# First product of the state tokens in three rounded products for chunks 1 to 3, with the batch sums moved to the front of a batch's last step

## The chip, the cores and the metric

One core of a Trainium2 chip runs the whole program. The metric is the device time of one execution in microseconds (us); the number that stands for a kernel is the median of several executions. One more execution was recorded by the hardware profiler, and all rows below come from it.

## The reference

Three layers follow each other. All inputs and outputs are fp32, and the kernel keeps fp32 accuracy.

```python
xread = softmax(scale * x @ state.T) @ state          # 4 batches, 8 heads, 512 tokens, D = 64
sread = softmax(scale * state @ x.T) @ x              # 32 state tokens per batch
x = concat([xread, sread])                            # 2304 tokens x 512
h = x @ w_in; g = softplus(h); x = g @ w_out          # first layer, d_ff = 2048
g = x @ w_gate; x = (silu(g) * (x @ w_val)) @ w_out2  # second layer, d_ff = 1536
```

Of the 2304 tokens 2048 come from `x` and 128 rows (4 batches x 32) come from `state`. Only these 128 state rows are touched by the first part of the change, and only in the product `x @ w_in`.

## The kernel before, in words

**Numbers in two parts.** A matrix is split into a high part (a float32r copy, made by ACT) and a low part (the rest, a subtraction on POOL or DVE, `low`, line 92). `mm3` (line 86) multiplies two split matrices with three float32r matmuls: high by high, low by high, high by low. A matmul on plain fp32 operands needs no split, and is recorded as two rows on PE.

**Weights** come as 64-bit words. A `Piece` of 128 x 512 goes through steps: a load (SP), `size` (ACT, line 132), `head` (DVE, line 136), `tail` (two integer passes on DVE, lines 143 and 146); these leave the fp32 tile `t_...`. Then come `high` (ACT, line 152) and `low` (POOL, line 92). Pieces of `w_in` end at `tail`; pieces of `w_out` go to the end. In between, pieces of the second layer (`gv`, `w`) are converted early and stored to memory; a `gv` piece is followed by four `sums` on POOL (line 193), a high part of them (`split_gv`, ACT, line 197) and a low part (POOL).

**The first layer** runs over four chunks c = 0 to 3 of 512 columns of d_ff, and in each over four batches b and four slices ft of 128: 64 units, 16 to a chunk and 4 to a batch. A unit has a first product `p1` (`ph`, six matmuls), the softplus twice (ACT `h` and `C`), their difference `l` (POOL, `g_low`), and a second product `p2` (`py`, twelve matmuls: four quarters dt of the output, three each). `p2` adds over the four slices of a batch in four PSUM banks; after a batch's last slice `y_add` (line 444) adds each quarter to `yacc` on DVE (line 453), which frees the bank.

**The order** is written by hand. The main loop goes over units n; at each step PE has `p2(n)`, the hooks called "pe", `p1(n + 4)`. Then ACT has `h` and `C` of the unit n + 3, and the other engines have their hooks: "dve0", "act", then `l`, "pool", "dve1", "act1". A table of hooks says at which step of a chunk something comes; each engine works through its own list in this order. SBUF slots and PSUM banks are given out by a planner, so more tiles of a kind can be alive than `bufs` says.

`p1` does not read the tokens' rows of w_in directly but a product `m` of state and w_in: `pm` (16 small matmuls, line 374) for the next chunk comes at steps 10, 12, 15 and 19 of a chunk (`M_STEPS`), with its high part on ACT and its low part on DVE one step later.

**The state tokens** go beside this, once per chunk: `s1` (line 502) multiplies `sw`, the 128 state rows, with the chunk's `w_in` in four plain fp32 matmuls (line 505) into `ps`; `s1_first` (line 508) takes the softplus, `sps`; `s2` turns it (`ptgs`), `s2_high` and `s2_low` split it into `gs`; `s3` (line 524) multiplies by `w_out` in twelve float32r matmuls, `ps<-wo,gs`; `s4` adds to `ys`. `s1` of chunk c + 1 stands at step 10 of chunk c, right behind `pm`; `s3` at step 20.

The lines of the main loop that the change moves:

```python
run(n, "dve0")
for dt in range(2) if last else ():
    y_add(u[0], u[1], dt)
run(n, "act")
if nx:
    g_low(nx)
run(n, "pool")
for dt in range(2, KT) if last else ():
    y_add(u[0], u[1], dt)
```

Of the kernel before, what the change touches and what calls it, by code (L numbers as in the profile page):

```python
# [9 lines left out]
F32R = mybir.dt.float32r  # L10
# [6 lines left out]
P = 128  # L17
# [16 lines left out]
FIRST = 9  # L34
# [3 lines left out]
def attention_moe_moe2_kernel(  # L38
# [36 lines left out]

    SLOTS = {"aT": 8, "mt": 8,  "wo": 6, "yacc": 8, "s": 2, "xT": 8, "T": 14, "made": 3, "w2": 4, "gw": 8}

# [162 lines left out]
    aT = {}  # L240
    sw = const.tile([P, KT, P], F32, tag="yo", name="sw")
    sr = {}
    srp = {}
# [118 lines left out]
    def st_out(b):  # L362
        v = srp[b][:, :P].rearrange("p (k s) -> p k s", k=KT)
        nc.scalar.activation(sw[:, :, b * NS:(b + 1) * NS], v, AF.Copy)


# [135 lines left out]
    def s1(c):  # L502
        ps = bank("m", f"ps1{c}")
        for kt in range(KT):
            nc.tensor.matmul(ps, sw[:, kt, :], win[c, kt].t, start=kt == 0, stop=kt == KT - 1)  # L505
        sp["s", c] = Softplus(ps, slot([P, CH], F32, "s", f"sps{c}"), None)
# [144 lines left out]
    with tc.manual_schedule(engines={ENG.PE}):  # L651
# [70 lines left out]
        def at_weights(n, late, store, key, make):  # L722
# [4 lines left out]
            for m, kind, step in (  # L727
                (n - 1, "act1", "size"), (n, "dve0", "head"), (n + late, "dve1", "tail"),
                (n + late + 1, "act", "high"), (n + late + 1, "pool", "low"),
            )[:3 if store is win else 5]:  # L730
                if m == FIRST - 1 and n == FIRST:
# [4 lines left out]
        for c in range(NCK):  # L736
# [15 lines left out]
            if c + 1 < NCK:  # L752
                for i, kind, fn in (
                    (10, "pe", s1), (11, "act", s1_first), (16, "pe", s2), (16, "act", s2_high), (17, "dve0", s2_low),
                    (20, "pe", s3), (21, "dve0", s4),
                ):
                    at(n0 + i, kind, fn, c + 1)
# [17 lines left out]
        for i in range(2):  # L775
# [4 lines left out]
            for k, t in ((0, "B22"), (1, "T1"), (2, "T3"), (3, "T2"), (4, "T4")):  # L780
                at(n0 + 2 * i + k, "act", y_high, 0, i, t)
                if t in ("T1", "T2", "T3"):
                    at(n0 + 2 * i + k + 1, "dve0", y_low, 0, i, t, nc.vector)
                else:
                    at(n0 + 2 * i + k, "pool", y_low, 0, i, t, nc.gpsimd)
        at(NU - 4, "pe", turn_ys)
        for n in range(2):
# [3 lines left out]
        with tc.manual_schedule(engines={ENG.DVE, ENG.SP, ENG.Activation, ENG.Pool}):  # L791
# [5 lines left out]
            for n in range(FIRST, NU):  # L797
# [10 lines left out]
                if nx:  # L808
                    sp[nx].high()
                    sp[nx].whole()  # L810
                last = u[2] == FT - 1
                run(n, "dve0")
                for dt in range(2) if last else ():
                    y_add(u[0], u[1], dt)
                run(n, "act")
                if nx:
                    g_low(nx)
                run(n, "pool")
                for dt in range(2, KT) if last else ():
                    y_add(u[0], u[1], dt)  # L820
                run(n, "dve1")
# [146 lines left out]
```

## Time and profile before

| what | value |
|---|---|
| median of 3 runs | 749.46 us (749.22 to 749.99) |
| the profiled execution | 746.57 us |
| its span | 744.8 us |
| mean granted clock of PE | 0.999 |
| busy: PE, POOL, DVE, ACT | 718.5, 384.4, 427.9, 321.5 us |
| first layer's `p2`, first to last | about 57 to 349 us |

PE is the row to read first: it is busy for 96% of the span. An idle stretch of another engine matters only if PE, or a chain that PE waits for, runs through it. Times such as 164.73 are microseconds from the start of the span.

### The profile page before, as it was taken

The page shows a single profiled execution, that of the slowest core. Times are in us where ns is not written, and L with a number is a line of the kernel's source. Part 1 is how long each engine was busy: PE and PEld are TensorE (multiplying, and loading weights), DVE is VectorE, ACT ScalarE, POOL GpSimd, SP SyncE. Part 2 cuts the span into 40 slices and gives each one's busy share as a digit, 9 for nine tenths or more (in the row PEclk, how much of TensorE's full clock was granted, in tenths as well). Part 3 has the DMA queues.
Part 4 walks back from the last instruction along what each step waited for, and adds up shares of the span by engine and source line. Part 5 has one row for each costly group of instructions (what it writes and reads, how often), then busy time and mean ns, then how long its engine had stood idle before and what let it go on. Part 6 is the DMA issues. An engine that isn't in the chain of part 4 may idle for free.

```text
span 744.8 us, 9985 instructions
## 1 busy us (share of the span) xinstructions
PE 718.5 (96%) x3640; PEld 566.9 (76%) x3640; DVE 427.9 (57%) x605; ACT 321.5 (43%) x586; POOL 384.4 (52%) x352
## 2 busy tenths in 40 slices
PE   5699999999999999999999999999999999999997
PEld 1367767776778777788788877888888888888885
DVE  5984558878666866467665555554644333333334
ACT  3766455543555454544543453442442232223221
POOL 2467637786648755744875566574442232223222
PEclk9999999999999999999999999999999999999999
DMA  9930224654545544460498988787455846255402
GB/s 337 408 118 5 80 86 141 199 198 169 168 143 177 191 127 157 164 260 1 165 378 295 333 326 310 255 320 244 142 198 184 274 174 226 88 200 205 161 1 113
DMA packets 51072, 143.78 MB, mean 193 GB/s; under 512 B 5712, under 2 KB 18000, under 8 KB 51024
## 3 DMA queue, kind: packets, MB, share of 16 engines
q1 hardware_dynamic: 51024, 143.15, 54.7%
q8 instruction: 28, 0.46, 0.2%
q14 instruction: 20, 0.16, 0.1%
HBM read 107.22 MB, written 35.91 MB: 192 GB/s over the span
## 4 chain that ended last, share of the span: by engine, by line
PE 82%; DVE 6%; DMA 4%; ACT 3%; POOL 3%; issue 2%; SPq 0%; ACTq 0%; DVEq 0%; POOLq 0%
PE py L89 24%; PE px L89 16%; PE po L89 16%; PE ph L89 10%; PE pz L89 7%; PE pt L89 3%; DMA gw<-gv_d 2%; PE ps L505 2%; PE pm L374 2%; DMA raw_gv<-in_moe_w_val_dram 2%; PE ps L89 1%; DMA st<-in_st_dram 1%; POOL sums_gv L193 1%; POOL gv L92 1%; DVE mx L273 1%
## 5 line engine op out<-in xcount | busy, mean ns | idle before, releaser
L89 PE MATMUL py<-h,wo 128*128 128x512 f32 x512 | 158.7, 390 | 2.3 <-DVE yacc L453 1.2
L92 POOL TENSOR_TENSOR l<-C,h 128x512 fp32r<-128x512 f32 x64 | 90.6, 1421 | 88.4 <-ACT C L407 71.7
L89 PE MATMUL po<-w,h 128*128 128x512 f32 x384 | 126.2, 391 | 0.0
L89 PEld LDWEIGHTS py<-h,wo 128*128 128x128 f32 x512 | 95.9, 188 | 23.6 <-POOL wo L92 1.9
L92 POOL TENSOR_TENSOR l<-cA,h 128x512 fp32r<-128x512 f32 x24 | 34.1, 1419 | 147.9 <-ACT h L574 147.9
L89 PE MATMUL ph<-aT,m 128*128 128x512 f32 x384 | 101.2, 399 | 1.5 <-ACT C L407 0.7
L89 PE MATMUL py<-l,wo 128*128 128x512 f32 x256 | 99.9, 390 | 0.1
L89 PEld LDWEIGHTS ph<-aT,m 128*128 128x128 f32 x384 | 70.7, 188 | 25.4 <-issue 6.9
L595 DVE TENSOR_TENSOR oacc<-po,oacc 128x512 f32<-128x512 f32 x80 | 55.1, 690 | 60.2 <-PE po L89 60.0
L404 ACT ACTIVATE h<-ph 128x512 fp32r<-128x512 f32 x64 | 38.2, 596 | 119.5 <-PE py L89 111.7
L89 PEld LDWEIGHTS po<-w,h 128*128 128x128 f32 x384 | 72.1, 188 | 14.9
L89 PE MATMUL po<-w,l 128*128 128x512 f32 x192 | 74.8, 390 | 0.5 <-POOL l L92 0.5
L89 PE MATMUL px<-T_0s,gw 128*128 128x512 f32 x216 | 61.3, 392 | 2.9 <-ACT cC L905 1.4
L89 PE MATMUL px<-T_1s,gw 128*128 128x512 f32 x216 | 60.7, 389 | 0.0
L89 PEld LDWEIGHTS py<-l,wo 128*128 128x128 f32 x256 | 48.0, 188 | 10.7 <-POOL l L92 0.5
L894 DVE TENSOR_TENSOR cA<-py,cA 128x512 f32<-128x512 f32 x24 | 16.6, 691 | 58.0 <-PE py L89 55.8
L89 PEld LDWEIGHTS px<-T_0s,gw 128*128 128x128 f32 x216 | 40.0, 188 | 12.8 <-ACT cC L905 2.3
L574 ACT ACTIVATE h<-cA 128x512 fp32r<-128x512 f32 x24 | 15.1, 631 | 77.7 <-DVE cA L913 77.7
L89 PEld LDWEIGHTS px<-T_1s,gw 128*128 128x128 f32 x216 | 40.5, 188 | 8.5
L905 ACT ACTIVATE cC<-px 128x512 f32<-128x512 f32 x24 | 14.3, 597 | 65.2 <-PE px L89 61.7
L89 PEld LDWEIGHTS po<-w,l 128*128 128x128 f32 x192 | 36.1, 188 | 8.2 <-POOL l L92 1.0
L92 POOL TENSOR_TENSOR l<-cC,h 128x512 fp32r<-128x512 f32 x24 | 31.9, 1327 | 15.4 <-ACT h L574 15.4
(148 smaller groups left out, 1321.5 us busy)
## 6 DMA issues: line engine op xcount, KB each, us to landing
gw<-gv_d SPq DMA_DIRECT2D x96, 512.0 KB, 6.7
gv_d<-gv SPq DMA_DIRECT2D x24, 512.0 KB, 3.1
gv_d<-split_gv SPq DMA_DIRECT2D x24, 512.0 KB, 3.5
w<-w_d SPq DMA_DIRECT2D x24, 512.0 KB, 9.0
raw_win<-in_moe_w_in_dram SPq DMA_DIRECT2D x16, 512.0 KB, 7.4
raw_wo<-in_moe_w_out_dram SPq DMA_DIRECT2D x16, 512.0 KB, 4.1
raw_gv<-in_moe_w_gate_dram SPq DMA_DIRECT2D x48, 128.0 KB, 4.1
raw_gv<-in_moe_w_val_dram SPq DMA_DIRECT2D x48, 128.0 KB, 3.7
```

The costliest lines, as they stand in the source:

```text
L89: nc.tensor.matmul(o, a[s], b[t], start=first and i == 0, stop=last and i == 2, **k)
L92: eng.tensor_tensor(out=o, in0=whole, in1=high.bitcast(F32), op=ALU.subtract)
L193: nc.gpsimd.tensor_tensor(out=o, in0=x, in1=y, op=op)
L273: nc.vector.tensor_reduce(out=self.mine("mx", 1), in_=self.sc, op=ALU.max, axis=AX.X)
L374: nc.tensor.matmul(ps[k * NS:(k + 1) * NS, :], st[q, k, b, :], win[c, k].t[q, :], start=True, stop=True)
L404: nc.scalar.activation(self.h, self.ps, AF.Softplus)
L505: nc.tensor.matmul(ps, sw[:, kt, :], win[c, kt].t, start=kt == 0, stop=kt == KT - 1)
L574: nc.scalar.activation(h, src, AF.Copy)
L595: nc.vector.tensor_tensor(out=v, in0=ps, in1=v, op=ALU.add)
L894: nc.vector.tensor_tensor(out=c["A"], in0=y, in1=c["A"], op=ALU.add)
L905: nc.scalar.activation(c["C"], x, AF.Copy)
```

## The change

It does four things. (1) For c = 1 to 3, `s1` uses `mm3` with `sws`, the high and low parts of `sw`, and with the high and low parts of the w_in pieces: twelve float32r matmuls in place of four fp32 ones. Chunk 0 stays as it is. (2) So `sw` is split once (ACT and DVE), and the twelve pieces of w_in get their `high` (ACT) and `low` (POOL), in four new SBUF slots; they come one step after a piece's `tail`, not before step 9. (3) `s1` goes from step 10 to 13, with its softplus, and `s2` to `s4` go one step later. (4) At a batch's last step all four `y_add` come ahead of the hooks "dve0".

```diff
--- before.py
+++ after.py
@@ -73,7 +73,7 @@
     psum = ctx.enter_context(tc.tile_pool(name="psum", bufs=1, space=bass.MemoryType.PSUM))
 
 
-    SLOTS = {"aT": 8, "mt": 8,  "wo": 6, "yacc": 8, "s": 2, "xT": 8, "T": 14, "made": 3, "w2": 4, "gw": 8}
+    SLOTS = {"aT": 8, "mt": 8,  "wo": 6, "yacc": 8, "s": 2, "xT": 8, "T": 14, "made": 3, "w2": 4, "gw": 8, "win": 4}
 
     def slot(shape, dt, tag, name):
         return slots.tile(shape, dt, tag=tag, bufs=SLOTS[tag], name=name)
@@ -239,6 +239,7 @@
 
     aT = {}
     sw = const.tile([P, KT, P], F32, tag="yo", name="sw")
+    sws = const.tile([P, 2, KT, P], F32R, name="sws")
     sr = {}
     srp = {}
     small = {}
@@ -362,6 +363,11 @@
     def st_out(b):
         v = srp[b][:, :P].rearrange("p (k s) -> p k s", k=KT)
         nc.scalar.activation(sw[:, :, b * NS:(b + 1) * NS], v, AF.Copy)
+
+    def split_sw():
+        v = sws[:, 0]
+        nc.scalar.activation(v, sw, AF.Copy)
+        low(nc.vector, sws[:, 1], sw, v)
 
 
     mt = {}
@@ -502,7 +508,13 @@
     def s1(c):
         ps = bank("m", f"ps1{c}")
         for kt in range(KT):
-            nc.tensor.matmul(ps, sw[:, kt, :], win[c, kt].t, start=kt == 0, stop=kt == KT - 1)
+            if c == 0:
+                nc.tensor.matmul(ps, sw[:, kt, :], win[c, kt].t, start=kt == 0, stop=kt == KT - 1)
+            else:
+                mm3(
+                    ps, [sws[:, i, kt, :] for i in range(2)], [win[c, kt].out[:, i, :] for i in range(2)],
+                    kt == 0, kt == KT - 1,
+                )
         sp["s", c] = Softplus(ps, slot([P, CH], F32, "s", f"sps{c}"), None)
 
     def s1_first(c):
@@ -727,7 +739,9 @@
             for m, kind, step in (
                 (n - 1, "act1", "size"), (n, "dve0", "head"), (n + late, "dve1", "tail"),
                 (n + late + 1, "act", "high"), (n + late + 1, "pool", "low"),
-            )[:3 if store is win else 5]:
+            ):
+                if store is win and step in ("high", "low"):
+                    m = max(m, FIRST + key[1] // 2)
                 if m == FIRST - 1 and n == FIRST:
                     m, kind = FIRST, "load"
                 if m >= FIRST:
@@ -751,8 +765,8 @@
                     at(n0 + i + 1, "dve0", m_pair_low, c + 1, b)
             if c + 1 < NCK:
                 for i, kind, fn in (
-                    (10, "pe", s1), (11, "act", s1_first), (16, "pe", s2), (16, "act", s2_high), (17, "dve0", s2_low),
-                    (20, "pe", s3), (21, "dve0", s4),
+                    (13, "pe", s1), (13, "act", s1_first), (17, "pe", s2), (17, "act", s2_high), (18, "dve0", s2_low),
+                    (21, "pe", s3), (22, "dve0", s4),
                 ):
                     at(n0 + i, kind, fn, c + 1)
         for i, kind, fn in (
@@ -783,6 +797,7 @@
                     at(n0 + 2 * i + k + 1, "dve0", y_low, 0, i, t, nc.vector)
                 else:
                     at(n0 + 2 * i + k, "pool", y_low, 0, i, t, nc.gpsimd)
+        at(FIRST, "act", split_sw)
         at(NU - 4, "pe", turn_ys)
         for n in range(2):
             at(NU - 5 + n, "load", load_gw, n)
@@ -809,15 +824,13 @@
                     sp[nx].high()
                     sp[nx].whole()
                 last = u[2] == FT - 1
+                for dt in range(KT) if last else ():
+                    y_add(u[0], u[1], dt)
                 run(n, "dve0")
-                for dt in range(2) if last else ():
-                    y_add(u[0], u[1], dt)
                 run(n, "act")
                 if nx:
                     g_low(nx)
                 run(n, "pool")
-                for dt in range(2, KT) if last else ():
-                    y_add(u[0], u[1], dt)
                 run(n, "dve1")
                 run(n, "act1")
                 run(n, "pool1")
```

**PE, chunk 1 of the loop, steps 10 to 13.** Before, `s1` (`ps`) stands between `pm` and the next `p1` (`ph`):

```order
L374 MATMUL pm_0_1_1842<-t_win_2_1567,st 32x512
L374 MATMUL pm_0_1_1842<-t_win_3_1629,st 32x512
L505 MATMUL ps_1847<-t_win_0_1385,sw 128x512
L505 MATMUL ps_1847<-t_win_1_1436,sw 128x512
L505 MATMUL ps_1847<-t_win_2_1567,sw 128x512
L505 MATMUL ps_1847<-t_win_3_1629,sw 128x512
L89 MATMUL ph_3_2_1853<-aT_0_938,m_3_0_1548 128x512 x3
L89 MATMUL ph_3_2_1853<-aT_1_940,m_3_1_1550 128x512 x3
L89 MATMUL py_2_0_1745<-h_2_3_1725,wo_3_1307 128x512 x2
```

And with the change, at the same place, and three steps on:

```order
L380 MATMUL pm_0_1_1877<-t_win_2_1596,st 32x512
L380 MATMUL pm_0_1_1877<-t_win_3_1645,st 32x512
L89 MATMUL ph_3_2_1882<-aT_0_939,m_3_0_1576 128x512 x3
L89 MATMUL ph_3_2_1882<-aT_1_941,m_3_1_1578 128x512 x3
...
L89 MATMUL py_3_3_1957<-l_3_1_1900,wo_1_1155 128x512
L89 MATMUL ps_2018<-win_0_1580,sws 128x512 x3
L89 MATMUL ps_2018<-win_1_1521,sws 128x512 x3
L89 MATMUL ps_2018<-win_2_1765,sws 128x512 x3
L89 MATMUL ps_2018<-win_3_1726,sws 128x512 x3
L89 MATMUL ph_0_1_2032<-aT_0_478,m_0_0_1896 128x512 x3
L89 MATMUL ph_0_1_2032<-aT_1_433,m_0_1_1898 128x512 x3
```

The four fp32 rows are gone from step 10, where `ph` now follows `pm`; four groups of three float32r matmuls stand at step 13, ahead of that step's `ph`.

**DVE and PE, chunk 1, end of the second batch** (`py_1_...` are the sums of that batch, `py_2_...` those of the next; `t_w` and `t_gv` are weights of the second layer). DVE before:

```order
L136 TENSOR_SCALAR t_w_1666<-t_w_1666 128x512
L143 SCALAR_TENSOR_TENSOR t_win_2_1567<-raw_win_2_1387,t_win_2_1567 128x512
L146 SCALAR_TENSOR_TENSOR t_win_2_1567<-raw_win_2_1387,t_win_2_1567 128x512
L143 SCALAR_TENSOR_TENSOR t_w_1666<-raw_w_1471,t_w_1666 128x512
L146 SCALAR_TENSOR_TENSOR t_w_1666<-raw_w_1471,t_w_1666 128x512
L136 TENSOR_SCALAR t_gv_0_1703<-t_gv_0_1703 128x512
L453 TENSOR_TENSOR yacc_0_953<-py_1_0_1571,yacc_0_953 128x512
L453 TENSOR_TENSOR yacc_0_953<-py_1_1_1572,yacc_0_953 128x512
L453 TENSOR_TENSOR yacc_1_955<-py_1_2_1573,yacc_1_955 128x512
L453 TENSOR_TENSOR yacc_1_955<-py_1_3_1574,yacc_1_955 128x512
```

DVE with the change:

```order
L549 TENSOR_TENSOR ys<-ps_1661,ys 128x512
L136 TENSOR_SCALAR t_w_1694<-t_w_1694 128x512
L143 SCALAR_TENSOR_TENSOR t_win_2_1596<-raw_win_2_1410,t_win_2_1596 128x512
L146 SCALAR_TENSOR_TENSOR t_win_2_1596<-raw_win_2_1410,t_win_2_1596 128x512
L143 SCALAR_TENSOR_TENSOR t_w_1694<-raw_w_1493,t_w_1694 128x512
L146 SCALAR_TENSOR_TENSOR t_w_1694<-raw_w_1493,t_w_1694 128x512
L459 TENSOR_TENSOR yacc_0_954<-py_1_0_1600,yacc_0_954 128x512
L459 TENSOR_TENSOR yacc_0_954<-py_1_1_1601,yacc_0_954 128x512
L459 TENSOR_TENSOR yacc_1_956<-py_1_2_1602,yacc_1_956 128x512
L459 TENSOR_TENSOR yacc_1_956<-py_1_3_1603,yacc_1_956 128x512
L136 TENSOR_SCALAR t_gv_0_1735<-t_gv_0_1735 128x512
```

The four `yacc` rows now come ahead of the head of `t_gv`, and `ys` stands here, a step later than it did. On PE the first second product of the next batch, with what it waits for, before:

```order
L89 MATMUL ph_2_3_1717<-aT_1_766,m_2_1_1366 128x512 x3
L89 MATMUL py_2_0_1745<-h_2_0_1608,wo_0_1203 128x512 [waits Activation_49]
L89 MATMUL py_2_0_1745<-h_2_0_1608,wo_0_1203 128x512
L89 MATMUL py_2_0_1745<-l_2_0_1662,wo_0_1203 128x512 [waits Pool_49]
L89 MATMUL py_2_1_1746<-h_2_0_1608,wo_0_1203 128x512 [waits DVE_49]
```

and with the change:

```order
L89 MATMUL ph_2_3_1749<-aT_1_767,m_2_1_1392 128x512 x3
L89 MATMUL py_2_0_1780<-h_2_0_1624,wo_0_1211 128x512 [waits DVE_49]
L89 MATMUL py_2_0_1780<-h_2_0_1624,wo_0_1211 128x512
L89 MATMUL py_2_0_1780<-l_2_0_1690,wo_0_1211 128x512 [waits Pool_49]
L89 MATMUL py_2_1_1781<-h_2_0_1624,wo_0_1211 128x512 [waits DVE_49]
```

The planner has dropped the fifth bank: before, the first quarter `py_2_0` waited for ACT only, and the second quarter for the bank that DVE's first `yacc` frees; now the first quarter itself waits for DVE.

**POOL, the same steps 15 to 23 of chunk 1.** Before:

```order
L92 TENSOR_TENSOR l_1_1_1498<-C_1_1_1459,h_1_1_1460 128x512
L92 TENSOR_TENSOR l_1_2_1554<-C_1_2_1493,h_1_2_1494 128x512
L92 TENSOR_TENSOR gv_0_1552<-t_gv_0_1469,gv_0_1552 128x512
L193 TENSOR_TENSOR sums_gv_0_1558<-t_gv_0_1469 128x128
...
L92 TENSOR_TENSOR split_gv_1_1658<-sums_gv_1_1624,split_gv_1_1658 128x512
L92 TENSOR_TENSOR l_2_0_1662<-C_2_0_1607,h_2_0_1608 128x512
L92 TENSOR_TENSOR l_2_1_1697<-C_2_1_1652,h_2_1_1653 128x512
L92 TENSOR_TENSOR l_2_2_1733<-C_2_2_1692,h_2_2_1693 128x512
L92 TENSOR_TENSOR w_1731<-t_w_1666,w_1731 128x512
```

With the change:

```order
L92 TENSOR_TENSOR win_1_1521<-t_win_1_1452,win_1_1521 128x512
L92 TENSOR_TENSOR l_1_2_1584<-C_1_2_1515,h_1_2_1516 128x512
L92 TENSOR_TENSOR win_0_1580<-t_win_0_1408,win_0_1580 128x512
L92 TENSOR_TENSOR gv_0_1582<-t_gv_0_1491,gv_0_1582 128x512
L193 TENSOR_TENSOR sums_gv_0_1589<-t_gv_0_1491 128x128
...
L92 TENSOR_TENSOR split_gv_1_1686<-sums_gv_1_1640,split_gv_1_1686 128x512
L92 TENSOR_TENSOR l_2_0_1690<-C_2_0_1623,h_2_0_1624 128x512
L92 TENSOR_TENSOR l_2_1_1728<-C_2_1_1681,h_2_1_1682 128x512
L92 TENSOR_TENSOR win_3_1726<-t_win_3_1645,win_3_1726 128x512
L92 TENSOR_TENSOR l_2_2_1769<-C_2_2_1720,h_2_2_1721 128x512
L92 TENSOR_TENSOR win_2_1765<-t_win_2_1596,win_2_1765 128x512
L92 TENSOR_TENSOR w_1767<-t_w_1694,w_1767 128x512
```

The low part of `win_0` stands ahead of the low part of `gv_0`, and that of `win_3` between `l_2_1` and `l_2_2`. Chunk 2 has the same rows; in chunk 0 the four new rows stand behind `l_3_0` and `l_3_1`.

## Rows read from the trace of the kernel before

**Rows 1.** The page: busy time by engine, and the costliest group with its idle time

```profile
PE 718.5 (96%) x3640; PEld 566.9 (76%) x3640; DVE 427.9 (57%) x605; ACT 321.5 (43%) x586; POOL 384.4 (52%) x352
...
L89 PE MATMUL py<-h,wo 128*128 128x512 f32 x512 | 158.7, 390 | 2.3 <-DVE yacc L453 1.2
```

**Rows 2.** The chain of waits, first layer: start us, us, what (chunks 1 and 2)

```profile
179.71 3.63 PE ps L505 x8
183.34 1.38 PE ph L89 x6
...
192.56 1.58 PE ph L89 x6
...
228.45 2.72 PE ps L89 x12
```

**Rows 3.** The same chain at the end of chunk 0

```profile
114.60 0.69 DVE m L92
...
115.34 1.66 PE ph L89 x6
```

**Rows 4.** Timeline of PE, chunk 1: [idle before, and what ended it]

```profile
166.08 0.62 PE L89 MATMUL py<-h,wo 128*128 128x512 f32 x2
...
168.15 0.74 PE L89 MATMUL py<-h,wo 128*128 128x512 f32 x2 [1.23 <-DVE yacc L453]
```

**Rows 5.** The chain of waits that leads to this wait of PE

```profile
147.33 1.84 POOL gv L92
...
155.07 1.70 POOL gv L92
...
160.34 0.99 DVE t_w L136
...
163.07 1.66 DVE t_win L146
164.73 0.61 DVE t_w L143
...
165.97 1.52 DVE t_gv L136
167.50 0.61 DVE yacc L453
```

**Rows 6.** Low and high parts of the w_out pieces: xcount, ns min/median/max

```profile
L92 POOL TENSOR_TENSOR wo<-t_wo,wo x16: 1279/1306/1749, 44.4 to 284.4; 128x512 fp32r<-128x512 f32 x16
...
L152 ACT ACTIVATE wo<-t_wo x16: 632/633/692, 43.5 to 282.9; 128x512 fp32r<-128x512 f32 x16
```

**Rows 7.** Timeline of POOL, chunk 1

```profile
161.00 3.17 POOL L92 TENSOR_TENSOR l<-C,h 128x512 fp32r<-128x512 f32 x2
165.92 1.29 POOL L92 TENSOR_TENSOR l<-C,h 128x512 fp32r<-128x512 f32 x1 [1.75 <-ACT C L407]
```

**Rows 8.** Timelines of DVE, POOL and PE, the same place in chunk 2

```profile
242.58 0.68 DVE L143 SCALAR_TENSOR_TENSOR t_w<-raw_w,t_w 128x512 int32<-128x512 int32 x1
...
243.90 0.42 DVE L136 TENSOR_SCALAR t_gv<-t_gv 128x512 int32<-128x512 int32 x1
244.24 2.48 DVE L453 TENSOR_TENSOR yacc<-py,yacc 128x512 f32<-128x512 f32 x4
...
238.93 3.17 POOL L92 TENSOR_TENSOR l<-C,h 128x512 fp32r<-128x512 f32 x2
244.45 1.31 POOL L92 TENSOR_TENSOR l<-C,h 128x512 fp32r<-128x512 f32 x1 [2.35 <-ACT C L407]
...
244.61 0.62 PE L89 MATMUL py<-h,wo 128*128 128x512 f32 x2
```

**Rows 9.** Timelines of DVE and PE at the first batch's end of chunk 3

```profile
298.08 2.73 DVE L453 TENSOR_TENSOR yacc<-py,yacc 128x512 f32<-128x512 f32 x4 [0.90 <-PE py L89]
302.68 2.74 PE py L89 x12
```

**Rows 10.** The page: issues of loads, KB each, median us from issue to landing

```profile
raw_win<-in_moe_w_in_dram SPq DMA_DIRECT2D x16, 512.0 KB, 7.4
```

## The prediction, made before the changed kernel ran

> **What bounds the kernel now.** I read the page first, for who is busy, then the chain of waits, for what the end hangs on, and then the timelines around the one wait that touches this change. PE is busy for 96% of the span, so time is won by taking work from PE or lost by making PE wait [rows 1]. The costliest group of the first layer shows the wait to look at: `py` stood 1.2 us for DVE's `yacc` [rows 1]. The chain of waits then runs along PE through nearly the whole first layer: the fp32 `s1` is in it for 3.63 us per chunk [rows 2]. It leaves PE for long only in chunk 1, at the end of the second batch: `gv` on POOL, its sums, the second `gv`, `t_w` on DVE, its passes, the head of `t_gv`, `yacc`, and then PE [rows 4, 5]. That is where the change puts new work.
>
> **The sum's base.** The profiled execution took 746.57 us; the median of the runs is 749.46 us, 2.89 us more. The terms below are differences, so I add them to the median. Times such as 165.97 are those of the rows; what PE itself gains is counted once, in the first term.
>
> **First product.** Taken out: 3.63 us of `s1` per chunk; the `ph` behind it took 1.38 us, where a `ph` right behind `pm` took 1.58 us, so 0.20 us come back [rows 2]. Put in: twelve float32r matmuls, the same count and width as `ps<-wo,gs`, which took 2.72 us [rows 2]. That makes -3.63 + 0.20 + 2.72 = -0.71 us per chunk, and three chunks **-2.13 us**. All of it lies on PE's path. If `ph` pays nothing extra, it is -2.73; if the new group pays 0.20 us as well, -1.53.
>
> **Step 13 of chunk 0.** `s1` of chunk 1 now comes where `ph` at 115.34 already stood for DVE's low part of `m`, which began at 114.60 [rows 3]. The bank that this low part frees now goes to `s1`, and `ph` follows it: the same wait with another waiter, **0**. The four low parts on POOL that `s1` needs cost at most 4 x 1.75 = 7 us [rows 6] and stand behind `l_3_0` and `l_3_1`, three steps ahead. Were that cover gone, PE would wait for one of them, 1.3 to 1.75 us.
>
> **New work beside PE.** POOL gets twelve low parts; the nearest row, the same subtraction for w_out, has 1.28 to 1.75 us, median 1.31 [rows 6]: 16 to 21 us in all. ACT gets thirteen copies of about 0.63 us [rows 6], DVE one subtraction of 0.69 us as in [rows 3]. Most lie in idle time of engines that are half empty [rows 1] and cost 0. Two of them per chunk, in chunks 1 and 2, don't.
>
> **The chain in chunk 1.** The low part of `win_0` stands on POOL ahead of that of `gv_0`, the start of the chain at 147.33 [rows 5]. So the chain begins 1.31 us late (1.28 to 1.75, [rows 6]). Some may come back: the two `gv` took 1.84 and 1.70 us [rows 5] where such a subtraction can take 1.28 [rows 6], 0.98 us in all, if they now miss the DVE passes beside them. Bounds 1.28 - 0.98 = 0.30 and 1.75; I take 0.9, with a little under half of it coming back.
>
> Next, `win_3`. DVE's passes on the weights slow down beside POOL: the `t_win` pass at 163.07 took 1.66 us while POOL worked through two `l` from 161.00 to 164.17 [rows 5, 7]; the `t_w` pass at 164.73 took 0.61 us with POOL idle until 165.92 [rows 5, 7]. Now `win_3` and then `l_2_2`, whose input is there at 165.92 [rows 7], fill that idle time. Both `t_w` passes may pay 1.66 - 0.62 = 1.04 us more, the 0.62 being half of 164.73 to 165.97 [rows 5]: 0 to 2.08; here I take 2.08, as both POOL instructions are ready.
>
> Against this, `yacc` no longer waits for the head of `t_gv` (1.52 us, [rows 5]), so it starts at 165.97 + 0.9 + 2.08 = 168.95 in place of 167.50. But the first quarter of `py`, which ran at 166.08 in a fifth bank [rows 4], must now wait too. From the start of `yacc` to PE it was 168.15 - 167.50 = 0.65 us [rows 4, 5]; a quarter of twelve matmuls takes 2.72 / 4 = 0.68. So the second quarter comes at 168.95 + 0.65 + 0.68 = 170.28, where it came at 168.15: **+2.13 us** (from 165.97 + 0.30 + 1.33 = 167.60, -0.55, to 165.97 + 1.75 + 2.08 + 1.33 = 171.13, +2.98).
>
> **The same place in chunk 2.** PE did not wait here: the first quarter ran at 244.61, and the first `yacc` at 244.24 freed the next bank just in time [rows 8]. Now the first quarter needs `yacc`, which follows the `t_w` passes that ended at 243.90 [rows 8]. Late by 0.9 from `win_0`; the first pass pays 1.04 beside `win_3`, as POOL's two `l` ended at 238.93 + 3.17 = 242.10, just ahead of the pass at 242.58; the second one I leave unpaid, since the next `l` has its input only at 244.45 [rows 8]. 243.90 + 0.9 + 1.04 + 0.65 = 246.49 against 244.61: **+1.88 us** (from 243.90 + 0.30 + 0.65 = 244.85, +0.24, to 243.90 + 1.75 + 2.08 + 0.65 = 248.38, +3.77).
>
> What the Trainium skill makes of this: its page "SBUF — State Buffer", section "Who interferes with whom", says that a VectorE instruction with two SBUF inputs and a GpSimd instruction that reads SBUF share one port pair, and that the one that starts first holds it while the other fully blocks. The 0.61 and 1.66 us above agree with that. By it a pass would be held only to the end of the POOL instruction, and the sum would come out 0.2 us lower, an estimate from that page's rule and the same rows.
>
> **The rest of the order.** At the other batch ends `yacc` is early enough: in chunk 3 it stood 0.90 us for PE, and its first bank, free at 298.08 + 0.69, was wanted only at 302.68 [rows 9]; a fifth bank isn't missed there: 0. At step 11 the low part of `m` now comes after the four `yacc`, up to 2.48 us later [rows 8], with a whole `p2` (2.72 us, as the twelve of [rows 2]) before its reader: 0, and up to 2.48 a chunk if that cover fails. `ys` and `gs` come a step later; the next reader is a whole step or more away: 0. Loads: SP changes little, and the planner gives the raw tiles of the weights one slot less; a load lands 7.4 us after its issue [rows 10] and is issued four steps ahead, about 16 us of matmuls: 0.
>
> **The sum.** -2.13 + 2.13 + 1.88 = **+1.88 us**, 748.45 on the profiled execution and 749.46 + 1.88 = **751.3 us** on the median. What a measurement of this kernel can tell from no change is about 0.2%, 1.5 us, so a slowdown just past that.
>
> **Rivals.**
> - **Batch ends don't bind: faster.** The chain gets back the 0.98 us and the `t_w` passes run at 0.62 us: -2.13 - 0.55 + 0.24 = -2.44, **747.0 us**. For it: `yacc` no longer stands behind 1.52 us of `t_gv` [rows 5]. Against it: between `gv` and `t_w` POOL and ACT hand the work to each other with no idle time that could take up 1.31 us. It decides where both places together cost no more than 2.13 - 1.5 = 0.6 us.
> - **Only one slow pass in each place: no change.** If `l_2_2` comes late enough in chunk 1 too, that term is 1.04 smaller: -2.13 + 1.09 + 1.88 = +0.84, **750.3 us**. If no pass is slowed and only the 0.9 us of `win_0` counts, it is -2.13 + 0.05 + 0.84 = -1.24, 748.2 us. For it: a pass that starts while POOL is between two instructions took 0.61 [rows 5]. Against it: 165.92 lies ahead of where the second pass now starts [rows 7].
> - **Both passes slow in chunk 2 as well: slower still.** +1.04, **752.3 us**. For it: 244.45 is within 0.3 us of the end of `win_3`.
> - **The saving isn't there**: `s1` at step 13 waits for `win` or splits badly. Then the first term is nearer -1.5, and the sum +2.5, 752.0 us. I see nothing for it but the moved bank [rows 3].
>
> **How the numbers follow.** Forecast and its slower neighbours (751.0 to 752.6): 0.45. One slow pass or none, 748.0 to 750.9: 0.35. Batch ends don't bind, below 748.0: 0.20. So faster 0.20, the same 0.35, slower 0.45. The range goes from 747.3, inside the faster case, to 752.6, past both slower rivals; about 0.1 lies below, and 0.1 above it, up to the 754.1 that both upper bounds would give.
>
> **What would show it.** Right: `ps<-win,sws` x12 of about 2.72 us and no line of fp32 `ps` after chunk 0; `py` waiting for `yacc` twice, in chunk 1 and chunk 2, 2 to 4 us each in the list of PE's waits; in the chain, the low part of `win_0` ahead of `gv`, and `t_w` passes of 1.6 us. Wrong: no such wait in chunk 2 (the first rival), or a new wait of `ps` or `ph` on POOL in chunk 0, or waits in chunk 3, which I price at 0.

## The result and the profile after

The changed kernel is slower: 755.2 us median (754.03 to 756.06, 4 runs) against 749.67 us (749.22 to 749.99, 4 runs, one more than above) for the kernel before, a ratio of 1.0088 with an interval of 1.0062 to 1.0113. The profiled execution took 754.03 us with a span of 752.0 us. The span of before was 744.8 us, so the two profiles differ by 7.2 us where the medians differ by 5.5: the profiled execution of before, 746.57 us, was quicker than its four timed ones. What follows compares the two profiles, one execution each. (The rows of the two inputs, 2048 and 128, make 2176 tokens, not the 2304 given above; nothing below depends on it.)

The page, busy time and the costliest group, as in [rows 1]:

```profile
PE 720.2 (96%) x3652; PEld 570.7 (76%) x3652; DVE 441.3 (59%) x606; ACT 328.6 (44%) x599; POOL 403.4 (54%) x364
...
L89 PE MATMUL py<-h,wo 128*128 128x512 f32 x512 | 160.3, 394 | 8.2 <-DVE yacc L459 3.6
```

PE is busy for 1.7 us longer, although its new product is the shorter one: a stretch at half clock, shown below, counts as busy. POOL is busy for 19 us and DVE for 13 us more. POOL got twelve subtractions; DVE got one, so nearly all of its 13 us is the same passes taking longer. The group of second products now stands idle for 8.2 us where it was 2.3. PE's waits in the first layer (what waited, for what, us in total, times, longest):

```profile
PE py L89 <- DVE yacc L459: 3.6, 3, 3.2
PE py L89 <- ACT w L152: 3.4, 1, 3.4
PE ps L89 <- DVE m L92: 0.9, 1, 0.9
PE py L89 <- POOL wo L92: 0.4, 1, 0.4
```

Where they stand is in PE's timeline, one line from chunk 0, one from chunk 1 and one from chunk 2, at the places of [rows 3], [rows 4] and [rows 8]:

```profile
112.13 3.03 PE L89 MATMUL ps<-win,sws 128*128 128x512 f32 x12 [0.86 <-DVE m L92]
...
169.33 0.73 PE L89 MATMUL py<-h,wo 128*128 128x512 f32 x2 [3.15 <-DVE yacc L459]
...
249.78 1.19 PE L89 MATMUL py<-h,wo 128*128 128x512 f32 x2 [3.41 <-ACT w L152]
```

The last one names ACT's copy of `w`, which ended last, at 249.70; DVE's first `yacc` ended at 249.65. Both come directly behind the second `t_w` pass. The chain of waits leads to both places (start us, us, what):

```profile
146.86 1.29 POOL win L92
148.15 1.44 POOL gv L92
...
160.84 1.07 DVE t_w L136
...
163.65 1.67 DVE t_win L146
165.31 1.71 DVE t_w L143
...
168.60 0.69 DVE yacc L459
...
195.76 2.72 PE ps L89 x12
...
227.46 1.29 POOL win L92
228.75 1.71 POOL gv L92
...
241.21 1.07 DVE t_w L136
...
245.68 1.70 DVE t_w L143
247.40 1.65 DVE t_w L146
```

`win` now stands ahead of `gv` in the chain, and in chunk 2, which the chain of before ran through on PE alone, it leaves PE in the same way. The `t_w` passes take 1.7 us. POOL's timeline in chunk 2 shows why:

```profile
245.09 1.73 POOL L92 TENSOR_TENSOR win<-t_win,win 128x512 fp32r<-128x512 f32 x1
246.77 1.71 POOL L92 TENSOR_TENSOR l<-C,h 128x512 fp32r<-128x512 f32 x1
248.45 1.72 POOL L92 TENSOR_TENSOR win<-t_win,win 128x512 fp32r<-128x512 f32 x1
```

And that of DVE at the same time:

```profile
245.60 1.77 DVE L143 SCALAR_TENSOR_TENSOR t_w<-raw_w,t_w 128x512 int32<-128x512 int32 x1
247.40 1.63 DVE L146 SCALAR_TENSOR_TENSOR t_w<-raw_w,t_w 128x512 int32<-128x512 int32 x1
248.96 2.47 DVE L459 TENSOR_TENSOR yacc<-py,yacc 128x512 f32<-128x512 f32 x4
```

POOL is without a gap from 245.09 on; the two passes that took 0.68 us there before [rows 8] lie wholly beside it, and `yacc` comes behind them. Behind the wait is a second loss. The busy time by stretches (stretch, length, then busy us of PE, PEld, DVE, ACT, POOL, the granted clock, DMA share, GB/s):

```profile
249.70:251.00 1.30, 1.22 (x3) 1.05 (x4) 1.30 (x3) 0.57 (x1) 1.30 (x2) 0.50 0.00 0
251.00:252.00 1.00, 1.00 (x3) 0.77 (x3) 0.96 (x3) 0.00 (x0) 0.41 (x1) 0.50 0.00 0
252.00:253.00 1.00, 1.00 (x4) 0.75 (x3) 0.97 (x2) 0.00 (x0) 0.00 (x0) 0.51 0.77 307
253.00:254.00 1.00, 1.00 (x6) 0.82 (x5) 0.55 (x2) 0.00 (x0) 0.00 (x0) 1.00 0.97 274
```

For some 3.4 us after the wait PE ran at 0.50, the lower of its two levels, 1.2 GHz: three or four matmuls in a microsecond where six are usual. That is 1.7 us lost in addition to the 3.41, in this one execution.

A ledger follows from the starts and ends of the second products in the two timelines of PE. Each entry is by how much the changed kernel fell behind (+) or drew ahead (-) between two such products:

| stretch of the first layer | forecast | measured |
|---|---|---|
| chunk 0, with `s1` of chunk 1 at step 13 | -0.71 | +0.06 |
| end of the first batch, chunk 1 | 0 | +0.41 |
| end of the second batch, chunk 1 | +2.13 | +1.88 |
| third batch of chunk 1, with `s1` of chunk 2 | -0.71 | -0.21 |
| end of the second batch, chunk 2 | +1.88 | +5.20 |
| third batch of chunk 2, with `s1` of chunk 3 | -0.71 | -0.20 |
| sum | +1.88 | +7.14 |

The largest entry, chunk 2, is read from these rows of PE, the first two before and the last two with the change: 255.49 - 242.13 = 13.36 against 248.69 - 240.53 = 8.16.

```profile
240.53 0.62 PE L89 MATMUL py<-h,wo 128*128 128x512 f32 x2
248.69 0.62 PE L89 MATMUL py<-h,wo 128*128 128x512 f32 x2
...
242.13 0.62 PE L89 MATMUL py<-h,wo 128*128 128x512 f32 x2
255.49 0.62 PE L89 MATMUL py<-h,wo 128*128 128x512 f32 x2
```

So the first layer (from the last second product that waits for POOL's `wo`, at 60.53 before and 60.01 with the change, to the first product of the second layer) went from 288.71 to 295.83 us, 7.12 more; the ledger's entries are rounded. This length is called "first layer" below, and each experiment's is given, since its start differs by up to 2 us from profile to profile.

### The profile page after: what moved, and what is told of

Its sections match the earlier page's. It is cut to its first block, busy times and chain, and to the rows that moved or that the text cites. A ratio compares the mean times of both kernels' runs of the same rounds, so it can differ in the third digit from the quotient of the medians.

```text
span 752.0 us, 10025 instructions
## 1 busy us (share of the span) xinstructions
PE 720.2 (96%) x3652; PEld 570.7 (76%) x3652; DVE 441.3 (59%) x606; ACT 328.6 (44%) x599; POOL 403.4 (54%) x364
## 4 chain that ended last, share of the span: by engine, by line
PE 72%; DVE 10%; DMA 6%; POOL 5%; ACT 3%; issue 3%; SPq 0%; DVEq 0%; ACTq 0%; POOLq 0%
PE py L89 20%; PE px L89 15%; PE po L89 15%; PE ph L89 7%; PE pz L89 7%; DMA raw_gv<-in_moe_w_val_dram 4%; PE pt L89 3%; DMA gw<-gv_d 2%; PE ps L89 2%; POOL sums_gv L193 2%; POOL l L92 1%; POOL gv L92 1%; PE pm L380 1%; DVE t_win L143 1%; DVE t_wo L143 1%
## 5 line engine op out<-in xcount | busy, mean ns | idle before, releaser
L92 POOL TENSOR_TENSOR l<-C,h 128x512 fp32r<-128x512 f32 x64 | 92.2, 1447 | 74.1 <-ACT C L413 74.1
```

Source lines behind the costliest of these rows:

```text
L92: eng.tensor_tensor(out=o, in0=whole, in1=high.bitcast(F32), op=ALU.subtract)
```

## The experiments

Two accounts were open. **A**: the cost is that of two places, `win_0` ahead of `gv` and `win_3` beside the `t_w` passes, and goes if the parts go to other steps. **D**: POOL, ACT and DVE hand the conversions to each other with so little to spare in chunks 1 and 2 that the new parts cost wherever they go. Beside these stood the sums' new place and the new product itself. Where an expectation uses a further letter, it is for one of these: B for the sums, C for `s1` at its new step and what comes with it. All ratios are to the kernel before on the same chip, with the 95% interval.

**The sums back in their old place**

```diff
-                for dt in range(KT) if last else ():
-                    y_add(u[0], u[1], dt)
                 run(n, "dve0")
+                for dt in range(2) if last else ():
+                    y_add(u[0], u[1], dt)
...
                 run(n, "pool")
+                for dt in range(2, KT) if last else ():
+                    y_add(u[0], u[1], dt)
```

> The change, with y_add in the order of before (two after the dve0 hooks, two after the pool hooks). Theory A (the low parts of win_0 and win_3 on POOL make yacc late): the two waits at the end of the second batch stay, and grow by the head of t_gv that now stands ahead of yacc again (0.4 to 1.5 us each): 755 to 758 us, py waiting for yacc over 3 us in chunks 1 and 2. Theory B (the moved y_add and the bank that went with it cost the time): the waits fall back to the 1.2 us of before, 747 to 750 us.

Measured: 761.72 us, ratio 1.0189 (1.0172 to 1.0206); first layer 303.35 us. DVE's timeline in chunk 1:

```profile
168.79 1.49 DVE L136 TENSOR_SCALAR t_gv<-t_gv 128x512 int32<-128x512 int32 x1
170.20 2.47 DVE L459 TENSOR_TENSOR yacc<-py,yacc 128x512 f32<-128x512 f32 x4
```

And PE's:

```profile
171.03 1.19 PE L89 MATMUL py<-h,wo 128*128 128x512 f32 x2 [5.15 <-DVE yacc L459]
```

The head of `t_gv` is back ahead of `yacc`, and the waits are 5.15 and, in chunk 2, 4.67 us. PE ran at half clock for longer behind each, 6.8 us lost in all where the change lost 1.7. With the new parts in place, the sums in front save 7.5 us of the first layer: they are no part of the loss at the second-batch ends, but a repair of it. So B is out here; the total still came out above A's 755 to 758 us, which had no term for the longer half clock.

**The sums in front alone, on the kernel before**

```diff
-                run(n, "dve0")
-                for dt in range(2) if last else ():
+                for dt in range(KT) if last else ():
                     y_add(u[0], u[1], dt)
+                run(n, "dve0")
...
-                for dt in range(2, KT) if last else ():
-                    y_add(u[0], u[1], dt)
```

> The kernel before, with only the four y_add moved ahead of the dve0 hooks. Theory A: yacc follows the t_w passes at once, the wait of 1.2 us in chunk 1 shrinks to about 0.5, nothing else moves: 748 to 750 us. Theory B: new waits of py for yacc, in sum 3 us or more: 752 to 755 us.

Measured: 747.9 us (10 runs) against 747.48, ratio 1.0015 (1.0000 to 1.0030); first layer 288.66 us. Hardly any difference in the end, made of two: it gains 1.0 us at the second-batch end of chunk 1, and loses 0.85 in chunk 0, where `ph` now waits (PE's timeline):

```profile
116.90 1.65 PE L89 MATMUL ph<-aT,m 128*128 128x512 f32 x6 [0.93 <-DVE m L92]
```

This is the wait that the changed kernel has in `ps` (0.86), here without any new part or product. It is 0.19 in the run with the sums back. So it belongs to the sums.

**The new parts in the quieter steps 9 to 12 of chunks 1 and 2**

```diff
-                    m = max(m, FIRST + key[1] // 2)
+                    m = max(m, FIRST + key[1] // 2) if key[0] == 1 else (key[0] - 1) * UC + (9, 9, 10, 12)[key[1]]
```

> The change, with the high and low parts of w_in in chunks 1 and 2 made at steps 9, 9, 10 and 12 of the chunk (win_0 to win_3), behind the end of the second batch and ahead of s1 at step 13; the same work on the same engines. Theory A: the waits of 3.2 and 3.4 us and the slow stretch of PE after the second go, and the saving of the first product shows: 746 to 749 us. Theory B and theory C (s1 at step 13 and its followers cost the time): the place of the low parts doesn't matter, 753 to 756 us.

Measured: 756.54 us, ratio 1.0116 (1.0099 to 1.0133); first layer 297.26 us. The second-batch ends are free (0.25 us and none), as A says. In their place `py` waits 1.19 and 1.33 us at the third-batch ends, and `ps` 1.87 and 1.88 us for POOL's last `win`, with half clock behind both (PE's timeline in chunk 1):

```profile
199.83 0.50 PE L89 MATMUL ps<-win,sws 128*128 128x512 f32 x1 [1.87 <-POOL win L92]
```

A has the mechanism, and its cure failed: the wait moved.

**The new parts made, the product as before**

```diff
-            if c == 0:
+            if True:
                 nc.tensor.matmul(ps, sw[:, kt, :], win[c, kt].t, start=kt == 0, stop=kt == KT - 1)
```

The parts are made and not read.

> The change, with s1 of every chunk in plain fp32 again, still at step 13; the high and low parts of w_in and sw are made and not used. All theories: the first product costs 3.63 us in place of 2.72 and the ph behind it 1.38: 0.9 us more per chunk where PE sets the pace; in chunk 0 the wait for the low part of m may change by some tenths. 755 + 2 to 3 = 757 to 758 us, if the saving of 0.71 us per chunk was real; 755 if it was lost in waits.

Measured: 759.99 us, ratio 1.0154 (1.0113 to 1.0196); first layer 299.61 us, 3.78 more than with the change. Of that, 1.7 is one more stretch at half clock (3.4 us lost in all); the rest, 2.1, is the three products. So the saving is there, and it is small.

**One of the two places at a time, and both**

`win_0` one step earlier, behind `win_1`; `win_2` and `win_3` behind `w`, at step 7:

```diff
                     m = max(m, FIRST + key[1] // 2)
+                    if key[0] > 1 and key[1] in (0, 2, 3):
+                        m, kind = (key[0] - 2) * UC + UC + (2 if key[1] == 0 else 7), kind + "1"
```

The other two kernels have `(0,)` and `(2, 3)` in place of `(0, 2, 3)`.

> As the change, with only win_0 moved into its gap; win_2 and win_3 stay. Theory A, in two parts: without win_0 ahead of gv the chain begins 1.3 us earlier, so the waits fall from 3.2 and 3.4 us to about 2 each; the t_w passes beside win_3 still take 1.6 to 1.8 us. PE's slow stretch in chunk 2 goes with the shorter wait. Ratio about 1.002 to 1.004.

> As the change, with only win_2 and win_3 moved into their gap; win_0 stays ahead of gv. Theory A, in two parts: the t_w passes go back to 0.6 or 0.7 us each, so the waits fall by about 2 us to 1.0 to 1.5 each. Ratio about 1.000 to 1.002.

> The change, with low and high parts of win_0 in chunks 1 and 2 one step earlier, right behind win_1 (ahead of l_1_2, where POOL waits 2.9 us in the trace of before), and those of win_2 and win_3 behind w at the batch's last step (where POOL waits 3.0 us there): the same work, in gaps. Theory A (the low parts delay the chain to yacc, through POOL's list ahead of gv and beside the t_w passes): the waits of 3.2 and 3.4 us fall to 0.3 or less, no new ones, and the saving of the first product shows: ratio to before 0.996 to 0.999. Theory D (any twelve low parts on POOL cost the time, wherever they stand, since POOL's list is what PE waits for): other waits come in their place, ratio 1.006 or more.

| | median us | ratio | first layer | PE's waits at the batch ends of chunks 1 and 2 |
|---|---|---|---|---|
| `win_0` moved | 751.56 | 1.0055 (1.0034 to 1.0075) | 293.52 | first 0.59 and 0.23, both in chunk 1; second 0.91 and 2.18; third 0.78, chunk 1 |
| `win_2`, `win_3` moved | 756.47 | 1.0117 (1.0090 to 1.0144) | 295.23 | second 2.08 and 2.31; third 0.20, chunk 1 |
| all three moved | 756.08 | 1.0109 (1.0092 to 1.0127) | 297.67 | first 0.59 and 0.23, both in chunk 1; third 3.25 and 3.09 |

Each place carries a part of the wait, and with both relieved the second-batch ends no longer bind at all. The three ratios lie above what A expected, most of all for `win_2` and `win_3`. DVE's timelines there show why: without `win_3` the first `t_w` pass is back at 0.68 us, but the second still takes 1.68 (chunk 1) and 1.64 (chunk 2), now beside POOL's `l`, as `win_0` still makes the head late. And with all three moved the third ends bind. DVE's timeline there in chunk 1, with all three moved:

```profile
184.79 1.77 DVE L143 SCALAR_TENSOR_TENSOR t_gv<-raw_gv,t_gv 128x512 int32<-128x512 int32 x1
186.60 1.64 DVE L146 SCALAR_TENSOR_TENSOR t_gv<-raw_gv,t_gv 128x512 int32<-128x512 int32 x1
188.16 2.47 DVE L459 TENSOR_TENSOR yacc<-py,yacc 128x512 f32<-128x512 f32 x4
```

It is the picture of the changed kernel one batch later, with `t_gv` for `t_w` and POOL's `wo`, `l`, `wo` for `win`, `l`, `win`. The kernel with `win_0` alone moved comes out best of the three, though it clears neither place.

**All three moved, with the product as before**

```diff
-            if c == 0:
+            if True:
                 nc.tensor.matmul(ps, sw[:, kt, :], win[c, kt].t, start=kt == 0, stop=kt == KT - 1)
```

on the kernel with all three moved; the parts are again not read.

> As e8_both_gaps, but s1 of every chunk in plain fp32, still at step 13; the parts of w_in are made and not used. It measures the first product alone: PE has 3.63 us and no ph of 1.58 in place of 2.72: 0.9 us per chunk, 2.7 us more than e8_both_gaps.

Measured: 760.24 us, ratio 1.0175 (1.0154 to 1.0196). Here the waits (3.27 and 3.07) and the half clock (3.4 us) are those of its partner, so the pair tells the product's price cleanly: first layer 299.66 against 297.67, **1.99 us** for three chunks, 0.66 each, where 0.9 was expected: at step 13, not behind `pm`, the fp32 `s1` takes 3.43 us in the chain of waits, for the 3.63 of [rows 2]. At the same place of chunk 1 `ps` took 3.59 us there and 2.88 in its partner.

**The parts one chunk later, in the chunk that uses them**

```diff
-                    m = max(m, FIRST + key[1] // 2)
+                    m = max(m, FIRST + key[1] // 2) if key[0] == 1 else key[0] * UC + key[1] // 2
...
-                    (13, "pe", s1), (13, "act", s1_first), (17, "pe", s2), (17, "act", s2_high), (18, "dve0", s2_low),
-                    (21, "pe", s3), (22, "dve0", s4),
+                    (13 if c == 0 else 19, "pe", s1), (13 if c == 0 else 20, "act", s1_first),
+                    (17 if c == 0 else 22, "pe", s2), (17 if c == 0 else 22, "act", s2_high), (18 if c == 0 else 23, "dve0", s2_low),
+                    (21 if c == 0 else 26, "pe", s3), (22 if c == 0 else 27, "dve0", s4),
```

> The change with high and low parts of w_in for chunks 2 and 3 a whole stretch later: at steps 16 and 17, in the four steps of a chunk that convert no gv piece and have 2.7 to 3.3 us of idle POOL each in the trace of before; s1 at step 19 behind pm, s2 at 22, s3 at 26. Same work. Theory A (only what stands ahead of a late yacc costs): all twelve low parts are free there, waits of py 0.3 us or less, ratio 0.995 to 0.999. Theory D (POOL's whole list is what PE waits for, any place costs): waits of 2 to 3 us again, ratio 1.006 or more.

Measured: 751.38 us (6 runs), ratio 1.0049 (1.0032 to 1.0066); first layer 290.48 us. This is the lowest ratio with the whole change in it (its interval overlaps that of `win_0` alone moved), and still slower than before. It has one large wait left, in PE's timeline of chunk 2:

```profile
244.77 0.73 PE L89 MATMUL py<-h,wo 128*128 128x512 f32 x2 [3.33 <-DVE yacc L459]
```

PE lost nothing at half clock here. How the wait comes can be read in the trace and was not shown by an experiment: with `s1` ahead of `ph` at step 19, ACT stands 4.64 us until the second product behind that `ph`, the high part of `split_gv` behind it comes at 228.61, and POOL idles 3.25 us for it, at the head of the same chain.

**The same, with `s1` a step earlier in both places**

```diff
-                    (13 if c == 0 else 19, "pe", s1), (13 if c == 0 else 20, "act", s1_first),
+                    (12 if c == 0 else 18, "pe", s1), (13 if c == 0 else 18, "act", s1_first),
```

> As e10_next_chunk, with s1 of chunks 2 and 3 one step earlier, at 18, and that of chunk 1 at step 12 behind pm. In e10 the s1 at step 19 stood between pm and the ph that ACT's list waits for, so split_gv began 2.5 us late; at step 18 it stands ahead of pm. Theory A (only work that makes a batch end's yacc late costs, on POOL or through ACT's list): the wait of 3.3 us goes to 0.3 or less, that of ps for m (0.86) shrinks, nothing else appears; first layer about 286 to 287 us against 288.7, ratio 0.996 to 0.999. Theory D: the wait of 2 us or more comes back at another batch end, ratio 1.003 or more.

Measured: 756.12 us (6 runs), ratio 1.0091 (1.0070 to 1.0111); first layer 296.03 us. A miss: in chunk 0 `ph` waits 3.44 us for `m`, and the wait in chunk 2 is still 3.24, each followed by half clock (3.4 us in all). Moving `s1` by a step does not take that last wait away: in POOL's timeline `gv` itself now begins late (228.90 for 222.03, with PE about 4.1 us later there), one link further up the same chain. What would take it away stayed open.

**No low parts of w_in at all**

```diff
-                    ps, [sws[:, i, kt, :] for i in range(2)], [win[c, kt].out[:, i, :] for i in range(2)],
+                    ps, [sws[:, i, kt, :] for i in range(2)], [win[c, kt].out[:, 0, :] for i in range(2)],
...
                     m = max(m, FIRST + key[1] // 2)
+                    if step == "low":
+                        continue
```

The twelve subtractions are left out, and the third matmul reads the high part instead.

> The change without the twelve low parts of w_in on POOL; the third matmul of each product reads the high part in place of the low one, so PE, ACT and DVE have the same instructions and the state tokens' product is not the reference's. Theory A or D (the low parts on POOL cost the time, at whichever batch end they are late for): no wait of py above 0.5 us, no stretch at half the granted clock, ratio 0.995 to 0.998. Theory C (the moved s1, the copies on ACT or the lost bank cost it): waits of 1 us or more stay, ratio 1.004 or more.

Measured: 747.87 us (10 runs) against 747.69 (17), ratio 1.0012 (0.9996 to 1.0028); first layer 288.54 us, 7.3 less than with the change. PE's waits in its first layer:

```profile
PE py L89 <- DVE yacc L459: 1.7, 4, 1.0
PE ps L89 <- DVE m L92: 0.9, 1, 0.9
```

The ACT copies, the new product and the sums are all there, and no half clock. One wait, 0.97 us at the second-batch end of chunk 1, is above the 0.5 that A and D allowed; before it was 1.23. **The loss at the second-batch ends is the low parts on POOL.** What is left shows also that the saving of 2.1 us goes elsewhere: the 0.9 in chunk 0, and 0.5 us at each third-batch end, to which PE now comes sooner, without the 3.63 us of `s1` ahead of it [rows 2].

**The low parts on DVE instead, in its idle stretches**

```diff
         def low(self):
-            low(nc.gpsimd, self.out[:, 1, :], self.t, self.out[:, 0, :])
+            eng = nc.vector if self.tag == "win" and not self.name.startswith("win1") else nc.gpsimd
+            low(eng, self.out[:, 1, :], self.t, self.out[:, 0, :])
...
                     m = max(m, FIRST + key[1] // 2)
+                    if key[0] > 1 and step == "low":
+                        m, kind = (key[0] - 1) * UC + (4, 4, 8, 8)[key[1]], "dve1"
```

> The changed kernel with the eight low parts of w_in for chunks 2 and 3 moved from POOL to DVE, into two idle stretches of DVE: those of win_0 and win_1 behind the head of t_win_2 (in the changed kernel DVE stood idle for 1.41 us right there, before 153.94 us), those of win_2 and win_3 behind the batch sums and the head of t_wo_0 (idle for 1.15 us before 174.34 us). POOL's list in chunks 1 and 2 is then that of the kernel before. Theory A (it is POOL that is short, and its instructions beside DVE's passes): the waits at the second-batch ends go to under 1 us each, no half clock, first layer about 289 to 290 us as without low parts (288.5), 747 to 749 us, ratio 0.999 to 1.003. Theory D (any further link in these two chunks costs, on whatever engine, since DVE's list feeds POOL and ACT as well): eight subtractions of about 0.7 us plus what they push behind; waits of 2 to 4 us come back at another batch end, the third (t_gv and t_wo late), first layer 293 to 297 us, 752 to 757 us, ratio 1.005 to 1.012.

Measured: 751.89 us (6 runs), ratio 1.0059 (1.0043 to 1.0076); first layer 293.52 us, with waits of 2.19 and 2.18 us at the second-batch ends and half clock behind the first (1.7 us). The time lies at D's lower edge, the waits lie where D did not have them, and A's "under 1 us each" failed: POOL's list in these chunks is that of before, and the parts still cost. POOL's timeline in chunk 1:

```profile
165.74 1.36 POOL L92 TENSOR_TENSOR l<-C,h 128x512 fp32r<-128x512 f32 x1 [0.91 <-ACT C L414]
```

And DVE's:

```profile
165.30 0.68 DVE L143 SCALAR_TENSOR_TENSOR t_w<-raw_w,t_w 128x512 int32<-128x512 int32 x1
166.01 1.64 DVE L146 SCALAR_TENSOR_TENSOR t_w<-raw_w,t_w 128x512 int32<-128x512 int32 x1
```

The head of `t_w` began at 160.91, 0.57 us later than before [rows 5], with PE 0.11 earlier. That was enough for the second pass to fall beside POOL's `l`, which starts when ACT's `C` lets it (165.74; 165.92 before, [rows 7]), and to take 1.64 us. A delay of 0.57 came out of the passes as one of about 1.7 (they end at 167.65 for 165.97).

No kernel here beats the kernel before. For every place and engine tried the parts cost more than the product saves; whether another place would be free is not shown. The two that equal it leave out either the low parts or everything but the sums.

## Why the prediction was right and wrong

The direction was right, the chain was right, and the size was not: +1.9 us forecast, +5.5 measured on the medians and 7.2 on the spans, outside the range.

**First product: right.** `ps<-win,sws` took 2.72 us in chunks 1 and 2, as forecast from its sibling, and the pair with and without it in an otherwise equal kernel gives 0.66 us per chunk for the forecast 0.71.

**Chunk 1: right to 0.25 us, for the reasons given.** The head of `t_w` came 0.50 us later than in [rows 5], with PE itself 0.06 earlier there; I had 0.9 for this. From there the passes took 2.13 us more, for which I had 2.08: the end of the passes, where `yacc` starts, went from 165.97 to 168.60.

**Chunk 2: the step that failed most,** +1.88 forecast and +5.20 measured. Three parts of it were off:
- The chain. Here the head of `t_w` went from 238.26 to 241.21, 2.95 us, of which 1.60 are PE's own lateness at that point (242.13 for 240.53, the second product ahead). So 1.35 for my 0.9: the full price of `win_0`, nothing of which came back. In POOL's timeline this `win` also stood 0.48 us for ACT's high part, which I had at 0. DVE's row before:

```profile
238.26 0.99 DVE L136 TENSOR_SCALAR t_w<-t_w 128x512 int32<-128x512 int32 x1 [2.48 <-ACT t_w L132]
```

- "The second one I leave unpaid, since the next `l` has its input only at 244.45." The passes cost 2.11 us, not 1.04 (`yacc` at 248.96 for 243.90, less the 2.95). I compared the time of that input on the clock of before with a pass that I had myself moved later. In the changed kernel `l` stood ready behind `win_3` and another `win` behind it, so POOL left no gap for either pass. With these two, my own formula gives 243.90 + 1.35 + 2.11 + 0.65 = 248.01, 3.40 us after 244.61; the wait was 3.41. The rival of both passes slow in chunk 2 had this mechanism right.
- The clock. A term for what PE does after a long wait was missing in the sum and in all rivals: 1.7 us at half clock.

**Step 13 of chunk 0: failed.** "The same wait with another waiter, 0": it cost 0.77 us (+0.06 for -0.71), with `ps` waiting 0.86 for DVE's `m`. I had taken the wait as one that the bank shifts from `ph` to `ps`, but in the kernel before it was only about 0.1 us (in PE's timeline the matmul ahead of the `ph` at 115.34 ends at 115.25). The runs with the sums moved alone (0.93) and moved back (0.19) show that the rest comes with the sums. The twelve parts had no share in it: without low parts the wait is still 0.86. My fear there was POOL, and `ps` did not wait for POOL. DVE's timelines, before and with the sums alone moved, show how it comes:

```profile
103.43 0.69 DVE L451 COPY yacc<-py 128x512 f32<-128x512 f32 x1 [3.46 <-PE py L89]
...
104.15 0.69 DVE L451 COPY yacc<-py 128x512 f32<-128x512 f32 x1 [7.59 <-PE py L89]
```

Before, a low part of `m` and a head of `t_gv` stood ahead of the sums and filled time in which DVE has to wait for PE. Now they come behind the sums, and the next low part of `m`, two steps on, begins at 116.17 for 114.60, 0.85 us later against PE, which is 0.72 later there. I had priced the delay of `m` at 0 because its own reader has a whole `p2` of cover; DVE's list carried the delay on to the next `m`.

**The rest of the order: mis-sized.** The price 0 for the other batch ends missed 0.41 us at the first one of chunk 1, which is gone without low parts, and 0.5 us at each third one, which is not. I had judged whether `yacc` comes early enough by the time of PE in the kernel before; without `s1` ahead of the third end, PE comes there 3.4 us sooner (3.63 less 0.20, [rows 2]). That this alone is the cause was not tried. In chunk 3, loads, `ys` and `gs` there was nothing, as forecast.

Of the 5.3 us by which the sum of +1.88 fell short of 7.14, the second-batch end of chunk 2 has 3.3, chunk 0 has 0.8, the third ends 1.0, the first end 0.4, and chunk 1's -0.25 goes the other way.

## What to carry to other kernels

Before work goes to a half-idle engine, follow the chain that this engine feeds to the next place where PE waits for a bank, and reckon the new work there, not by the engine's share. Where a pass has two speeds, according to what runs beside it, redo the overlap with the shifted times: a delay of half a microsecond can put a whole pass beside another engine's work and triple in size. Work that moves to the front of an in-order list can leave its engine idle there; follow what it displaced to the next reader. And where PE is made to wait, add a term for half clock behind the wait: 0 or 1.7 us after the waits of 1.87 to 3.44 us measured here.

## What the runs showed that I had not expected

**Half clock after short waits.** A wait of PE of about 2 us in the middle of a busy kernel was often followed by some 3.4 us at a granted clock of 0.50, 1.7 us lost: after 3.41 us (chunk 2 of the changed kernel), after 2.08 and 2.31 (`win_2` and `win_3` moved), after 1.87 and 1.88 (the parts in steps 9 to 12). No wait of 1.33 us or less in these first layers was followed by it. After the 5.15 us with the sums back it lasted until about 177, by stretches:

```profile
171.00:172.00 1.00, 0.97 (x2) 0.83 (x3) 1.00 (x3) 0.00 (x0) 0.41 (x1) 0.50 0.00 0
172.00:175.00 3.00, 3.00 (x8) 2.34 (x7) 2.30 (x5) 0.00 (x0) 0.00 (x0) 0.50 0.44 178
175.00:177.00 2.00, 2.00 (x6) 1.63 (x5) 0.00 (x0) 0.90 (x2) 0.00 (x0) 0.52 0.68 258
177.00:180.00 3.00, 3.00 (x14) 2.45 (x14) 1.68 (x2) 1.25 (x3) 2.74 (x3) 1.00 0.00 0
```

But 3.15 us (chunk 1 of the changed kernel) and 3.33 us (parts one chunk later) were followed by full clock, and in one profile (the low parts on DVE) 2.19 us was followed by half clock and 2.18 was not. What decides it was not found; the length of the wait alone does not.

**Two engines slow each other.** A pass of DVE on 128 x 512 words took 0.68 us with POOL idle and 1.63 to 1.78 beside POOL; POOL's low part took 1.29 to 1.31 alone and 1.71 to 1.74 beside DVE. The Trainium skill, page "SBUF — State Buffer", section "Who interferes with whom", says that a VectorE instruction with two SBUF inputs contends with a GpSimd instruction that reads SBUF, and calls their shared port pair an exclusive lock. By this rule a pass is held to the end of POOL's instruction, and the timelines of chunk 2 agree: the pass begun at 245.60 ended at 247.37, 0.55 us after POOL's `win` (246.82), and the next one at 249.03, 0.55 after POOL's `l` (248.48), each a little less than the 0.68 of a pass alone. The 0.2 us less that the prediction drew from this rule did not come: the passes cost 2.13 and 2.11 us more, where 2.08 was the full price.
